# A transformer block on one core: row-half products of the projections recorded in two queues instead of one alternating order

## The chip, the cores and the metric

The kernel runs on one core of a Trainium2 chip. The metric is the device time of one execution in microseconds. Three runs of the kernel before gave 2015.23, 2015.58 and 2016.20 us; the median is 2015.58.

## The reference

One transformer block on 2048 tokens of width 640, in float32: pre-normalization, attention with 32 heads of width 20, output projection and residual, then a second normalization and a gated feed-forward of width 1728.

```python
def _A_ref(x, wqkv, wo):          # H = 32, Dh = 20
    qkv = (x @ wqkv).reshape(B, S, 3, H, Dh).transpose(2, 0, 3, 1, 4)
    q, k, v = qkv[0], qkv[1], qkv[2]
    scores = jnp.einsum("bhqd,bhkd->bhqk", q, k) * (Dh ** -0.5)
    p = _softmax(scores, axis=-1)
    o = jnp.einsum("bhqk,bhkd->bhqd", p, v)
    return o.transpose(0, 2, 1, 3).reshape(B, S, D) @ wo

h = x + _A_ref(_layernorm(x), wqkv, wo)
h2 = h + _B_ref(_layernorm(h), w_gate, w_up, w_down)   # (silu(z @ w_gate) * (z @ w_up)) @ w_down
```

The change is in `x @ wqkv` and in the maxima of the scores that the softmax needs.

## The kernel before

The program has three stretches: projections (the product with `wqkv`), attention, and the output projection with the feed-forward. Only the first is touched. Work there is recorded by hand, instruction by instruction; a small planner keeps an estimated time for each engine in `clock` (lines 201 to 213) and decides from it what is recorded next. On the chip each engine then runs its own instructions in the recorded order and waits on semaphores.

**Projections.** The 2048 tokens come in four chunks `c` of 512. For each chunk, ten blocks of 128 columns of queries and keys (`query_key`, products 512 columns wide) and eight half rows of values (`value`, 320 columns wide) are computed. The first chunk and chunks 1 and 2 do blocks, then values; the last does five blocks of keys, the values, five blocks of queries. To keep float32 accuracy, both operands are split into a high and a low part, and a result is the sum of 15 products: 5 slices `k` of the contraction times three pairs of parts.

Each of these products is cut along the contraction into rows 0 to 63 and rows 64 to 127 (`half(0)` and `half(1)` in `rounds`, line 643). The two run on the lower and the upper 64 rows of TensorE's array, and two products on different halves can run at the same time. Both add into the same PSUM bank, so the upper half may start on a bank only when the lower half has done all its 15 products there. This crossing goes through an empty instruction on VectorE (`clobber_nop`, line 648), which waits for the last lower product and tells TensorE. `rounds` records a lower product and puts its upper twin into the list `behind`; once more than `LAG = 20` twins are in that list, one twin is recorded after each lower product. Three banks (`ps_one`) hold blocks in work; `keep` and `keep_value` empty them, through ScalarE, VectorE and GpSimd, into DRAM.

**Maxima.** The softmax subtracts each score row's maximum. A part of these maxima is computed during the projections, between other products: 144 units, each for one tile of 128 queries and one chunk of 512 keys, for two pairs of heads. A unit of `max_four` takes two of five PSUM banks (`ps_max`), one for each half of the array, since two heads lie in the lower and two in the upper rows. It records four products of 256 columns with differences of keys (line 239), a Relu on ScalarE for each of the two banks (line 251), and, when the planner holds these to be done, four more products that add the keys themselves; then VectorE reduces each bank (line 261). The sum of Relu(a-b) and b is the larger of a and b, so one reduction of 512 columns covers 1024 scores. `visit`, called after each recorded product, starts units (list `early`), finishes them (`seconds`), and records the deferred splits, the normalization steps (`lns`) and the transposes of the next chunk's tokens (`flip`, line 569, three groups a chunk; ScalarE copies at line 575, GpSimd splits at lines 586 and 587).

When the maxima of the first unit of attention are complete, `max_all(0)` reduces them, and `max_finish(0)` transposes them on TensorE, splits them into two parts on ScalarE and VectorE, and writes them into rows of the queries by four DMAs. Later units of attention mostly take another way, with a transpose on VectorE and a round through DRAM (`max_parts`, `max_turn`, `max_load`).

**Attention** begins with line 1303 (scores), with maxima still to be computed by single products (line 274) and reductions (line 280).

Of the kernel before, what the change touches and what calls it, by code (L numbers as in the profile page):

```python
# [17 lines left out]
P = 128  # L18
# [26 lines left out]
def tile_block(ctx: ExitStack, tc: tile.TileContext, x, wqkv, wo, wg, wu, wd, out):  # L45
# [168 lines left out]
    def max_pair(mx, q, k, pair, t, kc, k0):  # L214

        banks = [ps_max() for _ in range(2)]
        for b, ps in enumerate(banks):
            rows = slice(b * ROW, b * ROW + NPART)
            nc.tensor.matmul(
                ps, q[rows, pair, t * P : (t + 1) * P], k[rows, pair, k0 : k0 + CH],  # L220
                start=True, stop=True,
            )
        done = takes("PE", 240)
        for b, ps in enumerate(banks):
            nc.vector.tensor_reduce(
                mx[:, b, pair, t, kc : kc + 1], ps, axis=AX.X, op=ALU.max
            )
            hold([takes("DVE", 600, done + 205) + 100])

    def max_four(mx, q, k, t, kc):  # L230

        banks = [ps_max() for _ in range(2)]
        half = CH // 2

        def products(cols, first):
            for pair in range(2):
                for b in range(2):
                    rows = slice(b * ROW, b * ROW + NPART)
                    nc.tensor.matmul(  # L239
                        banks[b][:, pair * half : (pair + 1) * half],  # L240
                        q[rows, pair, t * P : (t + 1) * P], k[rows, pair, cols],
                        start=first and pair == 0, stop=True, skip_group_check=True,
                    )

        until = [[1e9] for _ in banks]

        def differences():
            products(slice(half, CH), True)
            done = takes("PE", 240)
            for ps in banks:  # L250
                nc.scalar.activation(ps, ps, AF.Relu)  # L251
                takes("ACT", 478, done + 150)
            hold(*until)
            return clock["ACT"] + RELU

        def maxima():
            products(slice(0, half), False)
            done = takes("PE", 240)
            for b, ps in enumerate(banks):
                until[b][0] = takes("DVE", 600, done + 205) + 100  # L260
                nc.vector.tensor_reduce(  # L261
                    mx[:, b, :, t, kc], ps.rearrange("p (j n) -> p j n", j=2),
                    axis=AX.X, op=ALU.max,
                )

        return differences, maxima
# [98 lines left out]
    with tc.tile_pool(name="pa", bufs=2) as pa:  # L365
# [54 lines left out]
        def staged_keys(g, c, kc, k, q):  # L420
            def four(t):
                first, second = max_four(mxs[g * NC + c], items[q][3], items[k][3], t, kc)

                def last():
                    second()
                    for n in (k, q):
                        users[n] -= 1
                    load_items()
                    if (g, c, kc, t) == (0, 0, NC - 1, TPC - 1):
                        max_all(0)  # L430

                return first(), last
# [5 lines left out]
            for n in (k, q):  # L438
                users[n] += len(ts)
            return [(ready, lambda t=t: four(t)) for t in ts]  # L440

        AFTER = 5, 6

# [24 lines left out]
        seconds, steps_due = [], [0]  # L468
        LANDING, LANDING_FIRST, SLACK, GATE, APART = 8000, 14000, 0, 500, 2500
        flips = []  # L470
# [4 lines left out]
        def norm_step():  # L475
# [3 lines left out]
            if lns and lns[0][0] == "POOL":  # L479
# [4 lines left out]
                x_there[0] = max(clock["PE"], clock["POOL"]) + CHAIN  # L484

        def visit():

            load_items()
            pe = clock["PE"]
            if seconds and seconds[0][0] <= pe + SLACK:  # L490
                seconds.pop(0)[1]()
                return
# [5 lines left out]
            if flips and held[1][0] <= pe + SLACK:  # L498
                flips.pop(0)()
                return  # L500
            if held[1][0] > pe + SLACK or clock["ACT"] > pe + GATE:
                return
            if early and early[0][0]():
                seconds.append(early.pop(0)[1]())
# [50 lines left out]
        def flip(c, n):  # L555
            finish_splits()
            if n == 0:
                while lns:
                    norm_step()
                zs[c] = z_tiles(c)  # L560
            ks = range(2 * n, min(2 * n + 2, ND))
            columns = len(ks) * TPC * ROW
            banks = [ps_max() for _ in range(2)]
            done = takes("PE", 450 * len(ks), held[1][0])
# [53 lines left out]
        behind, splits, lns = [], [], []  # L618
        LAG = 20
        given = [0, 0, 0]  # L620

        def second_half():
            if behind:
                f, crossed, done = behind.pop(0)
                clock["PE"] = max(clock["PE"], crossed[0])
                f(1)
                if done:
                    done()

        def taken(columns, done=None):  # L630
            done = clock["PE"] if done is None else done
            return takes("ACT", 46 + 0.844 * columns, done + 350) + 150

        def rounds(ps, n_columns, operands, done):

            last = len(operands) - 1
            crossed = [0]
            clock["PE"] = max(clock["PE"], given.pop(0))
            for n, (a, b) in enumerate(operands):

                def half(i, n=n, a=a, b=b):
# [1383 lines left out]
```

## Time and profile before

| | us |
|---|---|
| median of three runs | 2015.58 |
| the profiled execution | 2017.19 |
| its span, first to last instruction | 2015.4 |
| first half-row product of the projections (line 643) | 20.86 |
| first product of attention (line 1303) | 317.86 |
| busy time of TensorE over the span | 2002.7 |

A row of the timeline gives start, duration (of a merged run: all of it), engine, line, operation, output and input tiles, shape and count; in brackets the idle time before it and what ended it. Rows of the chain of waits have start, length, engine, output tile and line. The duration of a product there includes the time that its results need to run out of the array, so neighbours overlap; the pace is read from the distance between starts. Busy times of TensorE are a union over both halves of the array: one busy half counts as a busy engine.

### The profile page before, as it was taken

Reading aid. Unit: us, or ns where it says so; the run is one execution under the profiler, and the core shown is the slowest. Engines: PE = TensorE matmul, PEld = TensorE weight load, DVE = VectorE, ACT = ScalarE, POOL = GpSimd, SP = SyncE. Lnnn points to the kernel's source line nnn. Section 1 sums busy time; section 2 is a strip of 40 time slices with the busy share of each in tenths; the row PEclk is TensorE's granted clock in tenths of the full one; section 3 lists DMA queues with packets and bytes.
Section 4 is the critical chain, followed back from the end, with each engine's and each line's share of the span. In section 5 each row is a group of like instructions: output and inputs, shape, how many; then the busy total and the mean of one; then the engine's idle time right before and its main releaser. Section 6 shows DMA issues by size and latency. Waiting matters only on the chain.

```text
span 2015.4 us, 40030 instructions
## 1 busy us (share of the span) xinstructions
PE 2002.7 (99%) x14354; PEld 1247.8 (62%) x14354; DVE 1603.9 (80%) x2806; ACT 1437.1 (71%) x2819; POOL 796.8 (40%) x1190
## 2 busy tenths in 40 slices
PE   9999999999999999999999999999999999999999
PEld 8999995333333333333333333345598888888888
DVE  5677778888888888888888988886387666676677
ACT  4678878999999999999999999986633222212221
POOL 7465423333443443343400011011156444754555
PEclk9999999999999999999999999999999999999999
DMA  7777563352634544535513022321159654974642
GB/s 252 255 251 264 179 204 86 117 150 92 190 104 135 159 128 133 160 122 164 172 40 88 22 75 71 94 63 56 40 185 312 223 187 154 354 274 156 206 150 94
DMA packets 199340, 310.35 MB, mean 154 GB/s; under 512 B 53744, under 2 KB 87856, under 8 KB 198120
## 3 DMA queue, kind: packets, MB, share of 16 engines
q1 hardware_dynamic: 192552, 284.21, 43.8%
q0 software_dynamic: 6496, 23.60, 3.9%
q8 instruction: 114, 1.87, 0.4%
q14 instruction: 82, 0.67, 0.1%
q10 hardware_dynamic: 96, 0.00, 0.0%
HBM read 208.11 MB, written 99.19 MB: 152 GB/s over the span
## 4 chain that ended last, share of the span: by engine, by line
PE 96%; DMA 1%; DVE 1%; POOL 1%; issue 0%; ACT 0%; SPq 0%; POOLq 0%; DVEq 0%; ACTq 0%
PE acc L1313 24%; PE ps_a L1481 17%; PE ps_one L1303 15%; PE ps_max L274 12%; PE ps_one L643 10%; PE ps_b L1576 9%; PE ps_max L239 3%; PE ps_max L1031 2%; PE ps_b L1031 2%; PE ps_two L805 0%; PE ps_two L696 0%; DVE mx L261 0%; DMA rb<-r_d 0%; DVE mx L280 0%; PE ps_max L1066 0%
## 5 line engine op out<-in xcount | busy, mean ns | idle before, releaser
L1309 ACT ACTIVATE probs<-ps_one 128x512 f32<-128x512 f32 x2048 | 1056.1, 612 | 61.9 <-PE ps_one L1303 35.0
L280 DVE TENSOR_REDUCE mx<-ps_max 128x1 f32<-128x512 f32 x1472 | 924.5, 683 | 107.0 <-PE ps_one L1303 73.2
L1303 PE MATMUL ps_one<-q_stk,k_stk 62*128 62x512 f32 x2048 | 580.6, 449 | 1.0 <-DMA q_stk<-m_d 1.0
L1313 PE MATMUL acc<-probs,v_stk 128*32 128x512 f32 x4096 | 546.3, 605 | 0.1
L1303 PEld LDWEIGHTS ps_one<-q_stk,k_stk 62*128 62x128 f32 x2048 | 248.0, 184 | 436.6 <-ACT probs L1309 413.9
L274 PE MATMUL ps_max<-k_stk,q_stk 60*128 60x512 f32 x1472 | 374.9, 426 | 1.1 <-DVE mx L261 0.9
L274 PEld LDWEIGHTS ps_max<-k_stk,q_stk 60*128 60x128 f32 x1472 | 272.5, 186 | 29.7 <-DVE mx L280 2.8
L1698 DVE TENSOR_TENSOR tmp<-ps_a,tmp 128x512 f32<-128x512 f32 x208 | 141.2, 689 | 121.0 <-PE ps_a L1481 94.0
L261 DVE TENSOR_REDUCE mx<-ps_max 128x2 f32<-128x512 f32 x288 | 180.6, 684 | 63.8 <-PE ps_max L239 60.2
L1313 PEld LDWEIGHTS acc<-probs,v_stk 128*32 128x32 f32 x4096 | 80.9, 108 | 179.8 <-issue 167.9
L251 ACT ACTIVATE ps_max<-ps_max 128x512 f32<-128x512 f32 x288 | 151.6, 583 | 42.8 <-PE ps_max L239 40.2
L1576 PE MATMUL ps_b<-halves,yp 128*128 128x320 f32 x1032 | 178.7, 308 | 0.2 <-DVE h L1581 0.2
L1576 PEld LDWEIGHTS ps_b<-halves,yp 128*128 128x128 f32 x1032 | 165.2, 188 | 16.0 <-DVE h L1581 0.5
L1481 PE MATMUL ps_a<-t,units 128*128 128x512 f32 x624 | 162.5, 396 | 0.0
L90 POOL TENSOR_TENSOR yp<-y,yp 128x256 fp32r<-128x256 f32 x96 | 60.4, 630 | 186.9 <-ACT yp L89 186.9
L1481 PE MATMUL ps_a<-z,units 128*128 128x512 f32 x516 | 133.9, 394 | 0.0
L1481 PEld LDWEIGHTS ps_a<-t,units 128*128 128x128 f32 x624 | 112.6, 188 | 18.5
L1348 POOL TENSOR_TENSOR o<-o,rb 128x512 f32<-128x512 f32 x31 | 39.9, 1286 | 199.8 <-DMA q_stk<-m_d 72.7
L1581 DVE TENSOR_TENSOR h<-ps_b,h 128x320 f32<-128x320 f32 x248 | 109.7, 480 | 5.8 <-PE ps_b L1576 4.3
L643 PE MATMUL ps_one<-z_hi,w_lo 64*128 64x512 f32 x380 | 113.3, 392 | 0.0
L643 PE MATMUL ps_one<-z_lo,w_hi 64*128 64x512 f32 x380 | 112.1, 392 | 0.0
L643 PE MATMUL ps_one<-z_hi,w_hi 64*128 64x512 f32 x380 | 111.5, 393 | 0.0
(224 smaller groups left out, 2651.7 us busy)
## 6 DMA issues: line engine op xcount, KB each, us to landing
units<-w_d SPq DMA_DIRECT2D x186, 256.0 KB
w_d<-stage SPq DMA_DIRECT2D x106, 256.0 KB
halves<-j_d SPq DMA_DIRECT2D x70, 320.0 KB
j_d<-stage SPq DMA_DIRECT2D x42, 320.0 KB
k_stk<-k_d SPq DMA_DIRECT2D x64, 160.0 KB
q_stk<-q_d SPq DMA_DIRECT2D x64, 160.0 KB
raw<-k_d SPq DMA_DIRECT2D x62, 160.0 KB
raw<-q_d SPq DMA_DIRECT2D x54, 160.0 KB
```

What stands on the lines that cost most here:

```text
L251: nc.scalar.activation(ps, ps, AF.Relu)
L261: nc.vector.tensor_reduce(mx[:, b, :, t, kc], ps.rearrange("p (j n) -> p j n", j=2), axis=AX.X, op=ALU.max,)
L274: nc.tensor.matmul(ps, queries[u][rows, pair, t * P : (t + 1) * P], keys[u // NC][rows, pair, kc * CH : (kc + 1) * CH], start=True, stop=True,
L280: nc.vector.tensor_reduce(mxs[u][:, b, pair, t, kc : kc + 1], ps, axis=AX.X, op=ALU.max)
L643: nc.tensor.matmul(ps, a[rows], b[rows], start=(i == n == 0), stop=(i == 1 and n == last), skip_group_check=True,)
L1303: nc.tensor.matmul(ps, keys[u // NC][rows, p, kt * P : (kt + 1) * P], queries[u][rows, p, :], start=True, stop=True,)
L1309: nc.scalar.activation(probs[p][:, b, :], ps, AF.Exp, scale=scale)
L1313: nc.tensor.matmul(acc[32 * j : 32 * j + 32, :], values[u // NC][:, kt, j * VW : j * VW + 32], probs[j // 2][:, j % 2, :], start=(kt == 0) ...
L1481: nc.tensor.matmul(ps.rearrange("p (t n) -> p t n", t=TPC), w[k][:, i], z[k][:, :, j], start=(first and m == 0), stop=(last and m == len(n ...
L1576: nc.tensor.matmul(ps, a, b, start=(n == 0), stop=(n == len(pairs) - 1))
L1581: nc.vector.tensor_tensor(out=h, in0=ps, in1=h, op=ALU.add)
L1698: add = lambda out, ps, x: nc.vector.tensor_tensor(out=out, in0=ps, in1=x, op=ALU.add)
```

## The change

Each half of the array gets a planned time of its own (`lane[0]`, `lane[1]`). After each lower product, `other_work` fills the half that is planned to be free earlier: the upper half with pending maxima of its own, or the next upper twin from `behind` if the planned crossing is past; the lower half with maxima of its own. The fixed distance of 20 is gone. A unit of maxima is cut into two, one for each half of the array, each with one bank, its own Relu and its own reduction (`max_half`); the numbers of products, Relus and reductions stay the same. A unit begins only when its bank is planned to be free and neither ScalarE (500 ns) nor VectorE (1200 ns) is planned to be too far behind. The crossing's empty instruction goes to the one of VectorE, ScalarE and GpSimd that is planned to be free first, and is recorded 200 ns after the planned end of the lower half's last product. Groups of token transposes are recorded only when the chunk's normalization steps are all recorded and 500 ns have passed on VectorE. The maxima of the first unit of attention take the way through DRAM, one step a block. An unused function is deleted.

```diff
-    def max_four(mx, q, k, t, kc):
-        banks = [ps_max() for _ in range(2)]
...
+    lane = [0, 0]
+
+    def spend(b, ns):
+        clock["PE"] = max(lane[b], clock["PE"])
+        lane[b] = clock["PE"] + ns
+        return lane[b]
+
+    def max_half(mx, q, k, t, kc, b):
+        half, until, own = CH // 2, [1e9], []
+        rows = slice(b * ROW, b * ROW + NPART)
+
+        def product(pair, cols, first):
+            nc.tensor.matmul(
+                own[0][:, pair * half : (pair + 1) * half],
+                q[rows, pair, t * P : (t + 1) * P], k[rows, pair, cols],
+                start=first and pair == 0, stop=True, skip_group_check=True,
+            )
+            return spend(b, 118)
+
+        def difference(pair):
+            if pair == 0:
+                own.append(ps_max())
+                hold(until)
+            done = product(pair, slice(half, CH), True)
+            if pair == 1:
+                nc.scalar.activation(own[0], own[0], AF.Relu)
+                return takes("ACT", 478, done + 150) + RELU
...
-            if flips and held[1][0] <= pe + SLACK:
+            if flips and held[0][0] <= pe and held[1][0] <= pe and not lns and flip_from[0] <= pe:
                 flips.pop(0)()
...
+            if not new or held[0][0] > pe + SLACK or clock["ACT"] > pe + GATE or clock["DVE"] > pe + GATE_DVE:
+                return False
...
+        def second_half():
+            if not behind:
+                return False
+            f, crossed, done, ns = behind[0]
+            if crossed[0] > max(clock["PE"], lane[1]):
+                return False
+            behind.pop(0)
+            f(1)
+            spend(1, ns)
...
+        def other_work(until=None):
+            while True:
+                visit()
+                if lane[1] < lane[0]:
+                    if not (maxima(1) or second_half()):
+                        lane[1] = min(lane[0], max(lane[1], clock["PE"]) + 60)
+                elif not maxima(0):
+                    if until is None or (until and until[0] <= lane[0] + 50):
+                        return
+                    if not (lane[1] <= lane[0] and (maxima(1) or second_half())):
+                        lane[0] += 60
...
-                    if (i, n) == (0, last):
-                        nc.vector.clobber_nop([nc.vector.lower_ap(ps)])
-                        crossed[0] = takes("DVE", 60, clock["PE"] + 450) + 50
+                def cross():
+                    name = min(("DVE", "ACT", "POOL"), key=clock.get)
+                    engine = {"DVE": nc.vector, "ACT": nc.scalar, "POOL": nc.gpsimd}[name]
+                    engine.clobber_nop([engine.lower_ap(ps)])
+                    crossed[0] = takes(name, 60, clock["PE"]) + 50
...
                 half(0)
-                takes("PE", 5 + 0.4427 * n_columns)
-                behind.append((half, crossed, done if n == last else None))
-                if len(behind) > LAG:
-                    second_half()
-                visit()
+                spend(0, ns)
+                if n == last:
+                    nops.append((lane[0] + 200, cross))
+                behind.append((half, crossed, done if n == last else None, ns))
...
+        finishing = [max_parts, max_turn, max_load]
+
+        def finish_first():
+            if of_first[0] == 0 and finishing:
+                finishing.pop(0)(0)
```

Three places show what moves on TensorE. First the head of the projections, right behind the first two blocks (which use all rows). The rows are merged; `ps_one` 400, 430 or 431, and 449 are the banks of the next three blocks, and a second appearance of a bank's first product (`z_hi`, `w_hi`) is its upper half. Before:

```order
L643 MATMUL ps_one_400<-z_hi_208,w_hi_154 128x512 x5
L643 MATMUL ps_one_400<-z_lo_209,w_hi_154 128x512 x5
L643 MATMUL ps_one_400<-z_hi_208,w_lo_155 128x512 x5
L643 MATMUL ps_one_431<-z_hi_208,w_hi_154 128x512 x5
L643 MATMUL ps_one_431<-z_lo_209,w_hi_154 128x512
L643 MATMUL ps_one_400<-z_hi_208,w_hi_154 128x512
L643 MATMUL ps_one_431<-z_lo_209,w_hi_154 128x512
L643 MATMUL ps_one_400<-z_hi_208,w_hi_154 128x512
```

Now:

```order
L680 MATMUL ps_one_400<-z_hi_208,w_hi_154 128x512 x5
L680 MATMUL ps_one_400<-z_lo_209,w_hi_154 128x512 x5
L680 MATMUL ps_one_400<-z_hi_208,w_lo_155 128x512 x5
L680 MATMUL ps_one_430<-z_hi_208,w_hi_154 128x512 x5
L680 MATMUL ps_one_430<-z_lo_209,w_hi_154 128x512 x5
L680 MATMUL ps_one_430<-z_hi_208,w_lo_155 128x512 x5
L680 MATMUL ps_one_449<-z_hi_208,w_hi_154 128x512 x2
L680 MATMUL ps_one_400<-z_hi_208,w_hi_154 128x512
L680 MATMUL ps_one_449<-z_hi_208,w_hi_154 128x512
L680 MATMUL ps_one_400<-z_hi_208,w_hi_154 128x512
```

The upper half's first product stood behind 21 lower ones and stands behind 32 now.

The second place is in the first chunk, where the lower half has begun the values (320 columns, the inputs `w_hi,z_hi` in this order) while the upper half is still in blocks (512 columns). Before:

```order
L643 MATMUL ps_one<-w_lo,z_hi 128x320
L643 MATMUL ps_one<-z_hi,w_hi 128x512
L643 MATMUL ps_one<-w_lo,z_hi 128x320
L643 MATMUL ps_one<-z_hi,w_hi 128x512
L643 MATMUL ps_one<-w_lo,z_hi 128x320
L643 MATMUL ps_one<-z_hi,w_hi 128x512
```

Now:

```order
L680 MATMUL ps_one<-w_lo,z_hi 128x320 x2
L680 MATMUL ps_one<-z_hi,w_hi 128x512
L680 MATMUL ps_one<-w_lo,z_hi 128x320 x2
L680 MATMUL ps_one<-z_hi,w_hi 128x512
L680 MATMUL ps_one<-w_lo,z_hi 128x320
L680 MATMUL ps_one<-z_hi,w_hi 128x512
```

One for one has become mostly two for one.

The third place is the token transposes of the first chunk, among its values. Before, the second group of 16 came 80 rows behind the first. Now:

```order
L680 MATMUL ps_one<-w_hi,z_hi 128x320
L616 MATMUL ps_max<-ident,xt 128x64 x16
L680 MATMUL ps_one<-w_hi,z_lo 128x320
L616 MATMUL ps_max<-ident,xt 128x64 x16
L680 MATMUL ps_one<-w_hi,z_lo 128x320
L227 MATMUL ps_max<-raw_156,raw_157 128x256 x2
```

The first group was recorded later and stands one product ahead of the second.

More of the change, by code (lines that the diff above doesn't have):

```diff
@@ L945, in tile_block @@
         store(queue=nc.sync)
-        if 0 in ends:
-            max_finish(0)
-        assert not early and 0 not in ends
+        while finishing:
+            finish_first()
+        assert 0 not in ends
     turn[0], last = 0, jobs[0]
```

154 lines of the change are left out of this document (75 added, 79 removed).

## The prediction

> **What bounds the kernel now.** I read the page's engine line first, then the busy time of each engine in four stretches (bounded by the first and last half-row product of the projections, and by the first and last attention product), then the chain of waits, and last the timeline of TensorE in the projections.
>
> ```profile
> PE 2002.7 (99%) x14354; PEld 1247.8 (62%) x14354; DVE 1603.9 (80%) x2806; ACT 1437.1 (71%) x2819; POOL 796.8 (40%) x1190
> 20.86:317.86 297.00, 293.44 (x3374) 277.33 (x3374) 215.04 (x362) 219.78 (x426) 153.61 (x211) 1.00 0.72 230
> 317.86:1456.70 1138.84, 1136.01 (x7909) 464.35 (x7906) 976.42 (x1644) 1075.32 (x2106) 334.00 (x549) 1.00 0.35 106
> ```
>
> The columns of the two stretches are length, then busy time of PE, PEld, DVE, ACT, POOL, then clock. TensorE is the bound, at clock 1.00, and the change touches only the 297.00 us from 20.86 to 317.86. There PE looks 99% busy, but that hides something: every product of this stretch uses 64 rows of the array, two such products can run at once, and a union of busy times counts the array as busy when only one half works. So I count each half by itself, with paces from rows.
>
> ```profile
> 300.43 0.93 PE ps_one L643 x8
> 301.36 0.25 PE ps_max L239 x4
> 78.40 0.30 PE L643 MATMUL ps_one<-w_hi,z_hi 64*128 64x320 f32 x1
> 78.43 0.30 PE L643 MATMUL ps_one<-w_lo,z_hi 64*128 64x320 f32 x1
> 78.55 0.31 PE L643 MATMUL ps_one<-w_hi,z_hi 64*128 64x320 f32 x1
> 78.70 0.30 PE L643 MATMUL ps_one<-w_hi,z_hi 64*128 64x320 f32 x1
> 141.39 0.53 PE L569 MATMUL ps_max<-ident,xt 64*128 64x64 f32 x10 [0.76 <-DVE xt L551]
> L643 PE MATMUL ps_one<-z_hi,w_hi x380: 383/392/502, 20.9 to 314.8; 64*128 64x512 f32 x190
> L643 PE MATMUL ps_one<-w_hi,z_hi x320: 301/306/410, 51.6 to 289.3; 64*128 64x320 f32 x160
> L239 PE MATMUL ps_max<-raw,raw x608: 272/278/392, 66.8 to 303.4; 60*128 60x256 f32 x152
> L239 PE MATMUL ps_max<-raw x544: 273/279/385, 45.6 to 317.9; 60*128 60x256 f32 x182
> ```
>
> Eight 512-column products take 0.93 us over both halves: 0.232 each on its half. 320 columns: 0.15 (78.40, 78.55, 78.70 are one half's), I use 0.147. Four maxima products of 256 columns take 0.25: 0.12 each. Ten of 64 columns in 0.53, less the 0.22 that one takes: some 0.06 to 0.07 on a half. Counts: three forms of 380 (1140, so 570 a half), three of 320 (480 a half), 608+544 = 1152 (576 a half), and 60 transposes a half. One half's work is 570x0.232 + 480x0.147 + 576x0.12 + 60x0.065 = 132 + 71 + 69 + 4 = 276 us. The lower half starts at 20.86, the upper one 20 products later, at 20.86 + 20x0.232 = 25.5, and the upper one ends the stretch. So the upper half stands idle for 317.9 - 25.5 - 276 = **16 us**, and that is what this change can move.
>
> **Where those 16 us are.** The upper half follows the lower at a distance of 20 products, whatever their width. Where a block of 512 columns meets values of 320 columns, the order still alternates one for one:
>
> ```profile
> 55.27 0.39 PE L643 MATMUL ps_one<-z_lo,w_hi 64*128 64x512 f32 x1
> 55.30 0.39 PE L643 MATMUL ps_one<-w_hi,z_hi 64*128 64x320 f32 x1
> 55.50 0.39 PE L643 MATMUL ps_one<-z_lo,w_hi 64*128 64x512 f32 x1
> 55.53 0.39 PE L643 MATMUL ps_one<-w_hi,z_hi 64*128 64x320 f32 x1
> ```
>
> The 320-column product is repeated after 0.23 us, not 0.147: its half loses 0.085 on each of 20 pairs, 1.7 us. Blocks turn to values four times (the lower half loses) and values to blocks four times (the upper loses): 4x1.7 = 6.8 us for each half. The other 9 us are waits that stop both halves:
>
> ```profile
> 99.39 0.84 ACT L89 ACTIVATE e<-e 128x768 fp32r<-128x768 f32 x1 [1.38 <-DVE e L737]
> 100.09 0.39 PE L643 MATMUL ps_one<-z_hi,w_hi 64*128 64x512 f32 x1
> 100.77 0.98 PE L239 MATMUL ps_max<-raw 60*128 60x256 f32 x4 [0.29 <-ACT ps_max L251]
> 110.28 0.87 PE L239 MATMUL ps_max<-raw 60*128 60x256 f32 x3 [0.59 <-ACT ps_max L251]
>   DVE xt L551: 3.9, 4
> 319.40 0.49 PE L274 MATMUL ps_max<-k_stk,q_stk 60*128 60x512 f32 x1 [0.93 <-DVE mx L261]
> ```
>
> At 99.39 ScalarE is late by a subtraction on VectorE, its copy of 0.84 holds a Relu, and the maxima product behind that holds all of TensorE. "DVE xt" is from the view of L569: transposes that wait for normalized tokens, 3.9 us in four records, of which each place counts twice (PE and PEld), so about 1.9. The last row is outside the stretch: attention's first maxima find no bank because VectorE still reduces.
>
> **The change part by part.** (1) *Own queue for each half.* No product is added or removed. Behind a place where widths meet, the new order puts two 320-column products beside one 512-column product, so the distance stays one of time: **-6.8**. It needs no engine other than TensorE.
>
> (2) *Head.* The new order issues 32 products of the lower half before the first of the upper, instead of 21. The rows:
>
> ```profile
> 24.48 1.44 PE L643 MATMUL ps_one<-z_hi,w_hi 64*128 64x512 f32 x8
> 30.95 0.69 DVE L90 TENSOR_TENSOR e<-ps_one,e 128x512 fp32r<-128x512 f32 x1 [0.67 <-ACT e L89]
> 31.69 0.50 PE L643 MATMUL ps_one<-z_hi,w_hi 64*128 64x512 f32 x1
> ```
>
> The upper half starts 11x0.232 = 2.55 us later, at 28.0; the first block is complete that much later, its emptying (which ends with the row at 30.95, and lets the row at 31.69 start) too, so the lower half waits for a bank to about 34.2. **+2.55**, less the 0.4 us that both halves lost before 31.69: **+2.1**.
>
> (3) *Token transposes.* They now wait in the recording until the normalization is recorded, and so lose their waits: **-1.9**, between 0 and -1.9. But in the first chunk the first two groups stand one product apart, and the third 4.0 us (by the paces above) ahead of the product that reads its tokens. GpSimd splits a group thus:
>
> ```profile
> 64.57 1.09 ACT L575 ACTIVATE e<-ps_max 128x512 f32<-128x512 f32 x2 [1.70 <-PE ps_max L569]
> 65.23 0.61 POOL L586 CAST z_hi<-e 128x512 fp32r<-128x512 f32 x1 [1.79 <-ACT e L575]
> 67.85 1.31 POOL L587 TENSOR_TENSOR z_lo<-e,z_hi 128x512 fp32r<-128x512 f32 x1
> 78.43 0.40 POOL L586 CAST z_hi<-v_stk 128x256 fp32r<-128x256 f32 x1 [1.23 <-ACT v_stk L575]
> 80.06 0.74 POOL L587 TENSOR_TENSOR z_lo<-v_stk,z_hi 128x256 fp32r<-128x256 f32 x1
> ```
>
> 65.23 to 69.16 is 3.9 us a group; two are 7.8, and the small third needs 1.55 until its second cast is through. From the first group's transposes to the reader lie 8.8 us of products; the chain needs 0.53 (transposes) + 0.66 (64.57 to 65.23, the first copy) + 7.8 + 1.55 = 10.5. **+1.7**, between 0 (if other waits stretch those 8.8 us) and 2.5. The later chunks leave 4 us and have no such pair.
>
> (4) *One bank a unit.* 288 Relus and 288 reductions stay. Each half's pair of products is followed by its own Relu, not by two:
>
> ```profile
> 101.71 0.51 PE L239 MATMUL ps_max<-raw 60*128 60x256 f32 x4
> 102.21 1.07 ACT L251 ACTIVATE ps_max<-ps_max 128x512 f32<-128x512 f32 x2 [0.50 <-PE ps_max L239]
> 103.34 0.52 PE L239 MATMUL ps_max<-raw 60*128 60x256 f32 x4
> 305.54 0.58 ACT L251 ACTIVATE ps_max<-ps_max 128x512 f32<-128x512 f32 x1
> ```
>
> Before: Relus start when the products end, take 1.07 for two, and TensorE goes on 0.06 later. Alone: the second product's 0.28, 0.58 and 0.06 = 0.92 us. In the new order the work between lies mostly between 0.92 and 1.4 us, so most Relus are covered, with about 0.1 us to spare. Late ones stop both halves, as at 100.09 above, where no L643 runs until the maxima product is released. The new gates on VectorE's backlog should save about half of the 2 us lost around 100 and 110 and some near 290; single late Relus cost it back: **0**, between -4 and +6.
>
> (5) *Crossing.* The empty instruction that tells the upper half that the lower is through with a bank now goes to whichever of three engines is free, and is placed later; in 20-odd blocks only 0.5 to 0.7 us of lower-half work cover it (at least 0.9 before, but for one). It needs the 0.39-0.23 = 0.16 that a product runs on, and two signals of about 0.06 (from 103.28 to 103.34): 0.3 if the engine is idle, up to 0.9 behind a Relu. **+1**, between 0 and 6.
>
> (6) *Finished maxima of the first unit* leave PE, ACT and DVE for two small GpSimd operations, one DVE transpose and five DMAs. The pair of DMAs is seen later:
>
> ```profile
> 928.03 4.82 DMA m_d<-turned
> 935.35 2.00 DMA q_stk<-m_d
> ```
>
> 7 us, and 40 reductions are still to come: at 297/288 = 1.03 us each 41 us of cover. SP's next loads (four of raw keys, and the values) stand behind the four loads and so up to 5 us later; if that cover failed, at most those 5 us. I take **0**.
>
> (7) *Attention's start.* The last upper-half run is 13 bare products, 3 us without maxima, so the 0.93 goes: **-0.9**.
>
> Sum: -6.8 + 2.1 - 1.9 + 1.7 + 0 + 1 + 0 - 0.9 = **-4.8 us**. The profiled execution took 2017.19 (span 2015.4, and 1.8 around it); its span would be 2010.6. The runs' median is 2015.58, 1.6 below the profiled one, and becomes **2010.8**.
>
> One rule bears on (4) and (5). In the Trainium skill, TensorEngine Tiling (Array Packing), Key Properties, tiles of the array operate independently; TensorE: Matmul & The Clock Gate, Part 3 "What overlaps and what doesn't", says products start strictly in program order. By the first alone a late Relu would cost one half only, and the sum would keep (4) and (5) near -2; the row at 100.77 follows the second.
>
> **Rivals.** *A: the waits go as well* (12%). If the gates also remove the roughly 7 us of other waits, the upper half runs from 28.0 nearly without a gap: 2001 to 2005, say 2003. For it: ScalarE and VectorE have 77 and 82 us free of 297. Against: they are late in bursts, not on average.
> *B: head and transposes eat it* (22%). Terms 3 to 5 near their upper bounds while the -6.8 holds: 2013 to 2018, say 2015. For it: nothing hides the head.
> *C: slower, by single waits in one program order* (17%). Each of 288 units stops both halves for itself. Without (4) the sum is -4.8; 4.8/288 = 17 ns a unit cancels it, and slower than 0.2% begins at (4.8+4)/288 = 31 ns. At 45 ns: 13 - 4.8 = +8, 2023.5. For it: the spare 0.1 us, with ScalarE copies of 0.84 in between. Against: the old order has a like margin for a pair, and its waits come to 9 us in all.
>
> **How the numbers follow.** The forecast's own case (2005 to 2012.5) has 49%. What a measurement of this kernel can tell from no change is 0.2%, 4.0 us. Faster: 43 of the 49, A's 12, 3 of B: 0.58. Same: 6 of the 49, 18 of B, 2 of C: 0.26. Slower: 1 of B and 15 of C: 0.16. Leaving out half of A below and half of C above, the range is 2002.5 to 2020.
>
> **What would show it.** In the new profile the first attention product should come near 314 instead of 317.86; mixed stretches should show two 320-column rows beside each 512-column row; the second half's first product should stand near 28.0; a wait of TensorE for GpSimd should show near 76 to 80; the token transposes (line 616 there) should have next to no idle time for DVE. The forecast is wrong if waits of the maxima products (line 227 there) for Relus add up to more than about 8 us, or if waits for the crossing show by name.

## The result, and the profile after

The changed kernel is slower. Each ratio below is to the kernel before on the same chip; 0.001 is 2.0 us.

| | kernel before | changed kernel |
|---|---|---|
| median of the runs, us | 2015.58 | 2031.67 (2028.0 to 2034.9) |
| ratio, 95% interval | | 1.0079 (1.0059 to 1.0098) |
| the same on a second chip | 2017.38 | 1.0069 (1.0052 to 1.0086) |
| profiled execution / its span | 2017.19 / 2015.4 | 2028.0 / 2026.2 |
| projections, first half-row product to first attention product | 297.00 | 309.34 |

The forecast was 2010.8, with 2002.5 to 2020 as its range. One execution of after_again and one of a_all3 took some 3730 us each; they are left out of the times and ratios below, and nothing here explains them. The busy times of the projections in the changed kernel, with the columns that the prediction explained:

```profile
20.78:330.12 309.34, 299.75 (x3371) 278.07 (x3371) 212.54 (x364) 221.53 (x425) 153.43 (x212) 0.99 0.68 220
```

All of the loss is in this stretch, which is 12.3 us longer. The span is only 10.8 us longer: from the first attention product to the first of the output projection it takes 1465.98 - 330.12 = 1135.86 us, where it took 1456.75 - 317.86 = 1138.89, and what follows takes 1.6 us more. PE's busy time in the projections grew, and yet there is more idle time: 309.34 - 299.75 = 9.6 us in which neither half works, where it was 3.6. Counted by half, as in the prediction, the upper half starts at 27.9 and starts its last product at 330.81, so it idles for 330.8 - 27.9 - 276 = 26.9 us (before: 16.4). That is 10.5 more idle time, and a start 2.4 later.

What is late is told by the chain of waits. Its shares by line from 20 to 331 us, first of the kernel before, then of the changed one:

```profile
by line: PE ps_one L643 67.9%; PE ps_max L239 20.6%; DVE mx L261 2.2%; PE acc L1313 1.5%; ACT ps_max L251 1.3%; PE ps_max L569 1.2%; PE ps_one L1303 0.9%; PE ps_max L274 0.9%; DVE v_a L99 0.6%; DVE xt L551 0.6%; issue 0.5%; DVE mx L280 0.4%
```

```profile
by line: PE ps_one L680 43.1%; PE ps_max L227 19.4%; DMA raw<-q_d 5.3%; issue 4.1%; POOL w_lo L90 3.9%; DVE mx L247 2.6%; DMA k_stk<-k_d 2.1%; DMA k_d<-z_lo 2.1%; POOL z_lo L634 1.9%; DMA raw<-k_d 1.7%; POOL k_d L662 1.7%; DMA xt<-in_A_x 1.
```

Over shorter windows the same view of the changed kernel has these pieces (start, length, what):

```profile
168.49 4.79 DMA xt<-in_A_x
...
173.30 3.98 DMA raw<-q_d
...
266.65 3.86 DMA k_d<-e
...
270.56 5.34 DMA raw<-k_d
...
277.20 6.64 DMA k_stk<-k_d
...
284.18 5.45 DMA raw<-q_d
```

Before, products are 88.5% of this stretch's chain (67.9 and 20.6) and no DMA is among its larger shares; after, they are 62.5%. The chain now runs through DMAs in two places: through a load of tokens and then one of raw queries up to 177.28, and from a store of keys through three loads, one behind the other on SP's queue, up to 289.63. Each piece is one transfer, from its issue to its landing. "raw" are the key and query chunks which the maxima products read. The timeline of the changed kernel, with TensorE at the ends of these chains, one row of VectorE and one of SP's queue:

```profile
175.88 0.35 PE L227 MATMUL ps_max<-raw 60*128 60x256 f32 x1 [2.36 <-DMA raw<-q_d]
177.27 0.35 PE L227 MATMUL ps_max<-raw 60*128 60x256 f32 x1 [0.66 <-DMA raw<-q_d]
279.49 0.35 PE L227 MATMUL ps_max<-raw 60*128 60x256 f32 x1 [0.33 <-DMA raw<-q_d]
281.13 0.47 PE L227 MATMUL ps_max<-raw 60*128 60x256 f32 x3 [1.29 <-DMA raw<-q_d]
282.66 5.16 SPq L176 DMA_DIRECT2D raw<-q_d  x8
287.89 0.22 DVE L273 TENSOR_REDUCE neg<-mx 128x16 f32<-128x64 f32 x1
288.94 0.35 PE L227 MATMUL ps_max<-raw,raw 60*128 60x256 f32 x1 [1.95 <-DVE neg L273]
289.82 0.47 PE L227 MATMUL ps_max<-raw,raw 60*128 60x256 f32 x3 [0.53 <-DMA raw<-q_d]
```

The brackets add up to 7.1 us. The row at 288.94 names a reduction on VectorE, but that had ended at 287.89 + 0.22 = 288.11, 0.8 us earlier; the eight query loads were issued up to 287.82, and they are the likelier releaser. No one transfer of the chain took 8 us, the time that the planner allows a load; the query load on which the chain has the products at 289.82 wait was issued only at 284.18, 5.6 us before them. So its issue was late too, behind the loads ahead of it on SP's queue. In all these waits both halves stand still, as the following windows show (length, busy time of PE, PEld, DVE, ACT, POOL, then clock):

```profile
176.00:178.00 2.00, 1.34 (x14) 1.14 (x16) 0.69 (x1) 0.76 (x2) 0.00 (x0) 1.00 0.63 184
...
286.00:290.00 4.00, 1.52 (x18) 1.17 (x16) 2.04 (x4) 0.82 (x2) 0.41 (x2) 1.00 0.72 274
290.00:292.00 2.00, 2.00 (x26) 2.00 (x27) 0.41 (x1) 1.76 (x4) 0.00 (x0) 0.80 0.64 226
292.00:300.00 8.00, 8.00 (x104) 7.95 (x102) 6.82 (x13) 6.26 (x13) 0.00 (x0) 0.84 0.66 220
```

After the last of them the granted clock is 0.80 and 0.84 for ten microseconds; as an estimate, 2 x 0.20 + 8 x 0.16 = 1.7 us of work are lost on top. Loads thus explain near 9 us. The rest has no such marks. The view of waits, of TensorE alone (total, times, longest), shows the loads at its head and many small waits below them:

```profile
PE ps_max L227 <- DMA raw<-q_d: 6.2, 7, 2.4
PEld ps_max L227 <- issue: 6.1, 5, 2.5
PEld ps_max L227 <- DVE mx L247: 2.7, 6, 0.8
PEld ps_max L227 <- ACT ps_max L240: 2.3, 8, 0.7
...
PEld ps_one L680 <- POOL z_hi L633: 0.4, 1, 0.4
PEld ps_one L680 <- ACTq L688: 0.4, 1, 0.4
```

The small rows do not tell the two kernels apart: for the reductions (2.7) and the Relus (2.3) the kernel before has 2.1 and 2.3 in the same places. But this view counts only time in which TensorE is quite idle; a maxima product that stops while products of the other half still run does not show in it.

### The profile page after: what moved, and what is told of

Read it like the earlier page. It is cut to its first block, busy times and chain, and to the rows that moved or that the text cites. A ratio compares the mean times of both kernels' runs of the same rounds, so it can differ in the third digit from the quotient of the medians.

```text
span 2026.2 us, 40040 instructions
## 1 busy us (share of the span) xinstructions
PE 2007.5 (99%) x14353; PEld 1248.7 (62%) x14353; DVE 1600.9 (79%) x2806; ACT 1438.2 (71%) x2818; POOL 796.5 (39%) x1192
## 4 chain that ended last, share of the span: by engine, by line
PE 93%; DMA 3%; POOL 2%; DVE 1%; issue 1%; ACT 0%; SPq 0%; POOLq 0%; DVEq 0%; ACTq 0%
PE acc L1361 25%; PE ps_a L1529 17%; PE ps_one L1351 16%; PE ps_max L260 13%; PE ps_b L1624 9%; PE ps_one L680 7%; PE ps_max L227 3%; PE ps_max L1079 2%; PE ps_b L1079 2%; DMA raw<-q_d 1%; POOL w_lo L90 1%; DMA xt<-in_A_x 1%; DVE mx L247 0%; PE ps_two L740 0%; DMA k_stk<-k_d 0%
## 5 line engine op out<-in xcount | busy, mean ns | idle before, releaser
L247 DVE TENSOR_REDUCE mx<-ps_max 128x2 f32<-128x512 f32 x288 | 180.8, 684 | 62.5 <-PE ps_max L227 59.3
L281 POOL CAST neg<-neg 128x16 fp32r<-128x16 f32 x23 | 4.5, 196 | 262.0 <-DVE neg L273 262.0
L1529 PEld LDWEIGHTS ps_a<-z,units 128*128 128x128 f32 x516 | 93.1, 187 | 16.0
L89 ACT ACTIVATE yp<-tmp 128x512 fp32r<-128x512 f32 x40 | 25.3, 632 | 103.2 <-POOL tmp L1617 103.2
```

The source lines that it names most:

```text
L247: nc.vector.tensor_reduce(mx[:, b, :, t, kc], own[0].rearrange("p (j n) -> p j n", j=2), axis=AX.X, op=ALU.max,)
L1529: nc.tensor.matmul(ps.rearrange("p (t n) -> p t n", t=TPC), w[k][:, i], z[k][:, :, j], start=(first and m == 0), stop=(last and m == len(n ...
```

## The experiments

Three theories. **T1**: raw loads are late, because a unit may be recorded 8 us after its loads' recording, and they really take longer on a queue that is not empty. **T2**: each unit has a bank, a Relu and a reduction of its own, and small lateness of each stops both halves. **T3**: the crossings, that is, the empty instructions that let the upper half into a bank, come late. The edits show changed lines alone, against the changed kernel unless said otherwise; three dots stand for lines between.

**Loads given 12 us instead of 8** (a_land12).

```
-        LANDING, LANDING_FIRST, SLACK, GATE, APART = 8000, 14000, 0, 500, 2500
+        LANDING, LANDING_FIRST, SLACK, GATE, APART = 12000, 14000, 0, 500, 2500
```

> The changed kernel with one number changed: a raw key or query load counts as usable 12 us after its issue, where it was 8 us, so that a maxima unit whose load is young is recorded later. Theory T1 (TensorE stands for raw loads that have not landed, near 173 to 177, 278 to 281 and 286 to 290 us, some 8 us in all, and the low clock after them): these waits go, and the time falls from 2031.7 to 2021-2026. Theory T2 (the loss is many small waits of single units for their own Relu or reduction, spread over the whole stretch): 2030-2034, no change. Theory T3 (the crossings): no change.

Measured: 2023.32, ratio 1.0026 (1.0016 to 1.0036). One number takes two thirds of the loss away, 1.0074 (the mean of the two ratios) - 1.0026 = 0.0048, 9.7 us. In its trace TensorE's larger waits are

```profile
PEld ps_max L227 <- ACT ps_max L240: 4.0, 11, 0.9
PEld ps_max L227 <- DVE mx L247: 2.7, 9, 0.7
...
PE ps_max L227 <- DMA raw<-q_d: 0.9, 1, 0.9
PE ps_max L227 <- DMA raw<-k_d: 0.5, 1, 0.5
```

The DMA rows shrink from 6.2 us to 0.9 and 0.5, and the row put down to VectorE (2.0) is gone. What is left by name are waits for Relus and reductions.

**More room behind each Relu and reduction, loads as they were** (a_margin).

```
-    RELU = 150
+    RELU = 400
...
-                until[0] = takes("DVE", 600, done + 205) + 100
+                until[0] = takes("DVE", 600, done + 205) + 350
```

> The changed kernel with 0.25 us more kept between a unit's Relu and its second products, and 0.25 us more between its reduction and the next use of a bank. T2: the waits of the maxima products for ScalarE and VectorE get rarer, and the time falls by 4 us or more, below 2028. T1: the waits for raw loads stay or move, 2028-2036.

Measured: 2027.52, ratio 1.0042 (1.0027 to 1.0057), some 6 us less. This alone does not show T2: maxima that are recorded later give their loads more time too, and in this trace the waits for raw queries are 2.9 us, shorter than in either trace of the changed kernel. A new wait for GpSimd's splits of the tokens appears (4.2 us, below). What T2 is worth is read from a_both.

**Crossing always on VectorE, at once, with more room** (a_dvecross).

```
-                    name = min(("DVE", "ACT", "POOL"), key=clock.get)
+                    name = "DVE"
...
-                    crossed[0] = takes(name, 60, clock["PE"]) + 50
+                    crossed[0] = takes(name, 60, lane[0] + 450) + 50
...
-                    nops.append((lane[0] + 200, cross))
+                    cross()
```

> The changed kernel with the empty instruction of the crossing always on VectorE and recorded right behind the lower half's last product, and 0.45 us more kept before the upper half follows, as the kernel before has it. T3 (late crossings stop both halves in blocks where only 0.5 to 0.7 us covers them): faster by 3 us or more, below 2028.5. T1 and T2: within 2 us of 2031.7.

Measured: 2033.18, ratio 1.0073 (1.0057 to 1.0090). No gain of the 3 us or more that T3 asked for can be seen. The intervals are wide, some 4 us on the difference, so a crossing cost of 1 us or so could hide there.

**First unit's maxima turned by TensorE again** (a_pemax).

```
-        finishing = [max_parts, max_turn, max_load]
+        finishing = [max_finish]
```

> The changed kernel with the first unit's finished maxima turned by TensorE and split on ScalarE and VectorE again, as before, in place of the path through DRAM. The prediction's term 6 says 0: within 2 us of 2031.7. Its upper bound (the loads behind the four loads stand up to 5 us later, and a maxima product waits for them): faster by 3 to 5 us.

Measured: 2029.69, ratio 1.0052 (1.0037 to 1.0067); the interval overlaps both of the changed kernel's. The waits for raw loads did not go away with the DRAM path: in this trace they are 7.7 us for queries and 2.2 for keys. Whether the path costs up to some 4 us (1.0074 - 1.0052) is left open; it is not what makes the loads late.

**The changed kernel once more** (after_again), beside the next three.

> The changed kernel once more, beside the three that follow: 2028 to 2035 if its waits for late loads vary from run to run (T1), and the gap to the kernel before again between 10 and 18 us.

Measured: 2030.0 to 2033.7, ratio 1.0069 (1.0052 to 1.0086), which agrees with the first measurement. Its DMA waits are 4.8 us for queries and 1.6 for keys, others than in the first trace: they vary between the two traces, as the times do.

**Both edits** (a_both): a_land12 and a_margin together.

> Both earlier edits: 12 us until a raw load counts as usable, and 0.25 us more behind each Relu and each reduction. If T1 and T2 are separate costs they add up: 8 us from the loads and some 4 us from the margins, 2019 to 2021. If the margins only moved what the loads already gave: 2022 to 2025. A wait of TensorE for GpSimd's splits in the second chunk, 6 us with the margins alone, would hold it at 2024.

Measured: 2018.77, ratio 1.0007 (0.9998 to 1.0017). Alone the edits gave 9.7 and 6.5 us; together they give 1.0074 - 1.0007, 13.5 us, nearly the sum that T1 and T2 said, and all of the loss. The same two windows of three traces: of the kernel before, with 12 us alone, then with both edits (the third number is the busy time of PE, the fourth that of PEld):

```profile
150.00:200.00 50.00, 50.00 (x577) 49.23 (x576) 39.26 (x72) 41.13 (x80) 24.80 (x40) 1.00 0.78 261
200.00:250.00 50.00, 50.00 (x639) 48.47 (x637) 38.58 (x62) 39.55 (x79) 21.00 (x27) 1.00 0.57 182
```

```profile
150.00:200.00 50.00, 49.85 (x575) 45.72 (x572) 41.61 (x74) 40.08 (x78) 21.50 (x36) 1.00 0.78 253
200.00:250.00 50.00, 50.00 (x638) 47.95 (x636) 41.78 (x66) 42.41 (x84) 23.92 (x31) 1.00 0.66 208
```

```profile
150.00:200.00 50.00, 50.00 (x616) 49.53 (x616) 42.90 (x77) 42.62 (x83) 22.99 (x38) 1.00 0.77 271
200.00:250.00 50.00, 50.00 (x654) 49.21 (x652) 42.35 (x67) 42.15 (x84) 23.14 (x29) 1.00 0.64 207
```

PE reads 49.85 or 50.00 throughout, so it shows nothing here. The busy time of the weight loads does: 93.7 of 100 us with 12 us alone, 97.7 before and 98.7 with both edits. A bare count of products would mislead, since it depends on their widths: the kernel before has 1216 and the version with 12 us alone 1213. Counted by width instead, with the prediction's paces, the two halves together have these 200 us filled with 186.1 us of work (314 products of 512 columns, 356 of 320, 473 of 256, 64 of 64) with 12 us alone. It is 193.8 in the kernel before (375, 336, 452, 49) and 196.5 with both edits (337, 379, 487, 64). So with both edits each half stands some 5 us less in these 100 us. This is where T2's waits were, one half idle beside the other. The two parts of a_margin, Relu and reduction, were not run one by one.

The largest wait left in this version is in one place, on the timelines of TensorE and of GpSimd:

```profile
84.08 0.49 PE L680 MATMUL ps_one<-z_hi,w_hi 64*128 64x512 f32 x1 [2.20 <-POOL z_hi L633]
...
86.92 0.68 PE L680 MATMUL ps_one<-z_hi,w_hi 64*128 64x512 f32 x1 [2.04 <-POOL z_hi L633]
```

```profile
77.66 0.61 POOL L633 CAST z_hi<-e 128x512 fp32r<-128x512 f32 x1 [12.31 <-ACT e L622]
...
86.47 0.40 POOL L633 CAST z_hi<-v_stk 128x256 fp32r<-128x256 f32 x1
```

GpSimd splits from 77.66 to 86.87 (the end of the last row) without a pause of note, after a wait of 12.31 us; the products that read the tokens wait for it twice.

**The head** (a_head): a_land12, and in the first blocks the crossing at once.

```
-                    name = min(("DVE", "ACT", "POOL"), key=clock.get)
+                    name = "DVE" if slot[0] < 3 else min(("DVE", "ACT", "POOL"), key=clock.get)
...
-                    crossed[0] = takes(name, 60, clock["PE"]) + 50
+                    crossed[0] = lane[0] + 1000 if slot[0] < 3 else takes(name, 60, clock["PE"]) + 50
...
-                    nops.append((lane[0] + 200, cross))
+                    cross() if slot[0] < 3 else nops.append((lane[0] + 200, cross))
```

> 12 us for the loads, and in the first blocks the crossing on VectorE recorded at once, so that the upper half follows after 20 lower products as in the kernel before. The prediction's term 2 (the head costs 2.1 us): 2 us below the kernel with 12 us for the loads alone, 2021.3 on the same chip, with the first upper product near 25.5 in place of 28.0. The rival: it is lost again at the next wait, no change.

Measured: 2022.26, ratio 1.0027 (1.0017 to 1.0037), against 1.0026. The upper half's first product comes at 25.65, as meant, and the time does not visibly move; the intervals leave room for some 3 us either way, so the 2 us of term 2 are not excluded by the times. The trace has the rival's sign: the 2.4 us were idle again later. By the starts of its products the upper half stands 1.2 us at 35.6, before a first product into a new bank, and 2.1 us at 62.8.

**The list not held up by the last keys** (a_order): a_land12, with

```
-        AFTER = 5, 6
+        AFTER = 5, 7
```

> 12 us for the loads, and the units of the last chunk's keys (first head group) are listed after those of head group 7, not 6, so that the list is not held up by keys that are not there yet between 259 and 279 us, while TensorE has no maxima. Theory: the empty stretch makes the rest crowd between 280 and 318, with 2 to 3 us of waits there; then 2020 to 2022. If the empty stretch costs nothing: 2023, or slower because the first unit's maxima finish later.

Measured: 2021.6, ratio 1.0023 (1.0014 to 1.0032): inside the first theory's band, but no different from a_land12 by the ratio. The empty stretch is gone (VectorE is busy 38.9 of the 50 us from 250 to 300, where a_land12 has 28.8), so no cost of it is seen. In the profiled run one wait of 3.56 us for a raw query load remains at 67.4; loads of the first chunks keep the allowance of 14 us that they had.

**Everything together** (a_all): both edits, the head, the order, and

```
-        flip_at = (12, 12, 12)
+        flip_at = (11, 12, 12)
```

> 12 us for the loads, 0.25 us more behind Relus and reductions, the early crossing in the first blocks, the last chunk's keys listed after head group 7, and the first token transposes of the second chunk offered one step earlier. With the margins and the 12 us together TensorE waits for nothing between 150 and 260 us, but 6 us for GpSimd's splits between 80 and 88 us. The token transposes are now recorded 8 us of lower-half work earlier, so these 6 us should go: 2011 to 2014, below the kernel before for the first time. Rival: the head's 2.5 us and the 6 us turn into other waits for VectorE or for a bank, 2017 to 2019 as with both margins alone.

Measured: 2012.81, ratio 0.9978 (0.9969 to 0.9987): faster than the kernel before by 4.4 us. The wait for GpSimd's splits is gone. Its attention starts at 314.19. What it still has is a crossing on GpSimd; TensorE's timeline, then GpSimd's:

```profile
53.12 0.40 PE L680 MATMUL ps_one<-z_hi,w_lo 64*128 64x512 f32 x1
56.67 0.49 PE L680 MATMUL ps_one<-z_hi,w_hi 64*128 64x512 f32 x1 [3.16 <-POOLq L688]
```

```profile
52.90 0.73 POOL L90 TENSOR_TENSOR z_lo<-z_lo 128x256 fp32r<-128x256 f32 x1
53.93 1.79 POOL L662 DMA_DIRECT2D k_d<-z_lo  x3 [0.30 <-POOL z_lo L90]
55.71 1.65 POOL L662 DMA_DIRECT2D q_d<-e  x3
```

The empty instruction stands behind a split and behind these stores but the last, which starts at 56.8, after the signal at 56.6. The issue of a DMA counts as no work of the engine, but its sequencer takes 0.5 to 0.6 us for each of these six.

**18 us for the first loads** (a_all3): a_all with

```
-        LANDING, LANDING_FIRST, SLACK, GATE, APART = 12000, 14000, 0, 500, 2500
+        LANDING, LANDING_FIRST, SLACK, GATE, APART = 12000, 18000, 0, 500, 2500
```

> The same with 18 us, not 14, until a raw load of the first chunk and a half counts as usable (loads were late near 63 us in some of the runs, by up to 4 us). If late first loads still cost in this version: 1 to 3 us below the one before it and a narrower spread of times. If not: the same within 1.5 us.

Measured: 2022.09, ratio 1.0022 (1.0010 to 1.0034). A miss: 9 us slower than a_all. Its trace has the crossing on GpSimd again (3.9 us), waits for Relus (2.2), a new one for ScalarE's copy of a block (2.3), and a DMA wait of 1.3, where a_all has none. By name that is some 4 us more than a_all; the rest of the 9 is not explained. So more room for loads is not better in itself. It also warns that one number, which records everything behind it anew, can move the time by 9 us. The causes given here therefore rest on waits that go in the trace as the time falls, not on the times alone.

**The same two edits in the kernel before** (b_both).

```
-    RELU = 150
+    RELU = 400
...
-                until[b][0] = takes("DVE", 600, done + 205) + 100
+                until[b][0] = takes("DVE", 600, done + 205) + 350
...
-        LANDING, LANDING_FIRST, SLACK, GATE, APART = 8000, 14000, 0, 500, 2500
+        LANDING, LANDING_FIRST, SLACK, GATE, APART = 12000, 14000, 0, 500, 2500
```

> The kernel before with the same two edits: 12 us until a raw load counts as usable, 0.25 us more behind each Relu and each reduction. If these margins only repair what the change broke (the old order already kept loads 7 us or more ahead and loses little at Relus): within 3 us of the kernel before. If both kernels have the same slack in them: faster by 4 us or more.

Measured: 2035.79, ratio 1.0091 (1.0078 to 1.0104), 18 us slower: a miss of both. Its windows and a row of its timeline:

```profile
318.00:331.00 13.00, 12.93 (x66) 9.76 (x65) 9.84 (x17) 8.46 (x16) 0.00 (x0) 0.50 0.04 13
```

```profile
312.20 6.11 PE L239 MATMUL ps_max<-raw,raw 60*128 60x256 f32 x31 [0.22 <-DVE mx L261]
```

With one queue and pairs, the added room puts maxima off until no products are left; from 307 to 333 us they stand alone, with waits for Relus and reductions between them. The order with a queue for each half absorbs the same room. Which of the two edits does the harm was not run.

**Crossing not on GpSimd** (a_nopool): a_all with

```
-                    name = "DVE" if slot[0] < 3 else min(("DVE", "ACT", "POOL"), key=clock.get)
+                    name = "DVE" if slot[0] < 3 else min(("DVE", "ACT"), key=clock.get)
```

> The fastest version so far (all edits, 14 us for the first loads), with the empty instruction of the crossing on VectorE or ScalarE only. In its trace TensorE waits 3.4 us at 53 us and 0.9 at 292 us behind a crossing that stands on GpSimd behind splits. Prediction's term 5 put a crossing at 1 us in all, between 0 and 6. Theory: these two waits go and nothing takes their place, 2008 to 2010, a ratio to the kernel before of 0.9960 +- 0.001. Rival: the next wait (for a bank, or for GpSimd's splits of the tokens) ends where they ended, 2012 to 2013.

Measured: 2011.55, ratio 0.9962 (0.9947 to 0.9976), the fastest, 7.7 us below the kernel before. The ratio fits the theory's 0.9960, the time lies between the two bands. Both waits are gone by name; a crossing on ScalarE of 0.4 us and two waits for raw loads of 0.9 us each have come, and the waits for Relus are 1.9 us as in a_all. The intervals of a_all and of this version overlap: the gain over a_all is not settled.

## Why the prediction was wrong, by its steps

The forecast of 2010.8 missed by 20.9 us. Of these the loads are 9.7 and the margins 3.8, by the runs above; the other 7 or so lie between the forecast and a_both, and are only in part named: 4.2 us for GpSimd's splits, and a low clock behind them.

**(1) Own queue, -6.8: right where it could be seen.** Two 320-column products stand beside one of 512 columns, as foretold:

```profile
271.96 0.39 PE L680 MATMUL ps_one<-z_hi,w_lo 64*128 64x512 f32 x1
271.97 0.45 PE L680 MATMUL ps_one<-w_hi,z_hi 64*128 64x320 f32 x2
272.19 0.39 PE L680 MATMUL ps_one<-z_hi,w_lo 64*128 64x512 f32 x1
```

That the time then falls by this much is not shown. a_nopool's -7.7 is of that size, but it has several other edits in it, and the queue alone was not run.

**(2) Head, +2.1: place and size right, effect not.** The first product of the upper half:

```profile
27.68 0.39 PE L680 MATMUL ps_one<-z_hi,w_lo 64*128 64x512 f32 x1
27.80 1.21 PE L680 MATMUL ps_one<-z_hi,w_hi 64*128 64x512 f32 x8
```

It stands between 27.68 and 28.0. But a_head took the delay away and gained nothing that its intervals can show; its trace has the time idle again at the next waits. A delay at the head is no cost of its own if something behind it waits anyway.

**(3) Token transposes, -1.9 and +1.7: the first right, the second right in place only.** The view of L616 has 0.6 us of waits for the transposes (by PE and PEld), none of them for normalized tokens. GpSimd's splits make TensorE wait 0.4 us by the list of waits, not 1.7, and near 84 us, not 76 to 80. The chain of two groups was the right place: with the margins it cost 4.2 us in two waits, more than the bound of 2.5.

**(4) One bank a unit, 0 (-4 to +6): the step that failed.** It said that "single late Relus cost it back", and counted Relus and VectorE's backlog only. The Relus and reductions cost more than the 0, though inside the bound of +6: margins are worth 3.8 us with the loads mended (1.0026 to 1.0007). But the larger part, 9.7 us, is an input that the step did not count at all: a maxima unit also needs its raw keys and queries. The prediction looked at SP's queue in term (6) alone, for the five DMAs of the first unit, and gave "at most those 5 us"; it read no row of the raw loads. The order of the units moved, the loads' allowance of 8 us did not, and the chain then has 5.34, 6.64 and 5.45 us for three loads one behind another, and 3.98 for one at 173.30. Nor did its signs of being wrong point there. Waits of the maxima products for Relus came to at most 3.0 us (2.3 by PEld and 0.7 by PE, in part the same places), well below the 8 that it named; a wait for the crossing did show by name, but only 0.4 us.

Why the old order had no such waits with the same 8 us was not run by itself. The kept traces show a difference in the issue of the loads. SP issues the same series at this place in both kernels: four loads of keys, four of queries, four of `k_stk`, four of keys, eight of queries. Before, it begins at 257.47 and pauses from 264.43 to 270.18; in the changed kernel it begins at 270.56, when a store of keys has landed, and no pause is above 1.4 us. The eight query loads, whose row in the changed kernel stands at 282.66 (above), were before

```profile
272.83 4.79 SPq L176 DMA_DIRECT2D raw<-q_d  x8
```

So the changed kernel's loads stand 9 to 14 us later and closer together. That this alone makes them late is not shown.

In the Trainium skill, DMA: Bandwidth & Descriptors, "Anatomy of one DMA — SWDGE (gpsimd) path", gives a transfer on GpSimd's path about 2 us and its bytes by 436 GB/s; these loads go through SP's, so the figure is only borrowed. One of these loads has at most 160 KB by the profile's view of DMA issues, so an estimate by that page is 2.4 us. The chain shows 3.98 to 6.64, with the DMA engines busy for 0.62 to 0.89 of the windows around: the measurement decides. In this kernel a load's allowance had to hold what stands ahead of it on the queue as well.

**(5) Crossing, +1: in keeping with the changed kernel** (0.4 us by name, and a_dvecross shows no gain, to within some 4 us). Its bound of 6 was not idle: a_all, with the other waits gone, has 3.16 us in one place.

**(6) First unit's maxima, 0: not settled**, as said at a_pemax.

**(7) Attention's start, -0.9: right for the wait that it named.** The first maxima of attention wait for nothing:

```profile
330.12 0.50 PE L1351 MATMUL ps_one<-q_stk,k_stk 62*128 62x512 f32 x1
330.45 0.40 PE L260 MATMUL ps_max<-k_stk,q_stk 60*128 60x512 f32 x1
```

Attention as a whole is 3.0 us shorter than before, and the cause of the other 2 was not looked for.

Rival C had the sign, and a part of the cause: single waits that stop both halves because products start in program order. It put all 13 us on waits of the units for their own Relus and banks; by a_both these are some 4 us. No rival named the loads, and A and B did not come.

## What to carry to other kernels

When the order of work moves, list every input of the moved work, loads among them, and compare each with the time that the order allows for it; a fixed allowance that was never tight may be the first to break. A union of busy times hides both idle halves and small waits: add up the products of a window by width, each at its own pace, and look at the busy time of the weight loads. And margins belong to an order: the same two numbers made one order 13 us faster and the other 18 us slower.

## What the runs showed of the hardware

The granted clock fell after waits, but not after each. One gap of 3.16 us in a_all, and one of 2.36 us in the changed kernel, left it at 1.00. Two gaps of 2.20 and 2.04 us with 0.80 us of work between them, in a_both at 84.08 and 86.92, were followed by half speed:

```profile
84.00:86.90 2.90, 0.80 (x6) 0.54 (x6) 0.69 (x1) 0.00 (x0) 2.71 (x5) 1.00 0.92 348
86.90:88.00 1.10, 1.08 (x8) 1.08 (x10) 0.00 (x0) 0.14 (x1) 0.73 (x1) 0.58 0.15 58
88.00:89.00 1.00, 1.00 (x11) 1.00 (x10) 0.87 (x2) 0.32 (x2) 0.00 (x0) 0.50 0.00 0
```

In the Trainium skill, TensorE: Matmul & The Clock Gate, "HAM oscillation — how this bites in real kernels", the rule is to leave no gap of TensorE above some 3.4 us. Here two shorter gaps were enough. The share of work is no rule by these traces either: 0.84 us of work in the 4.00 from 53 to 57 us of a_all left the clock at 1.00, and 1.52 us in the 4.00 from 286 to 290 us of the changed kernel were followed by 0.80. What decides stays open. In b_both the clock was 0.50 with PE "busy" for 12.93 of 13 us, with only 66 maxima products in those 13 us.
